# Splitting the first batch of a fused attention and MoE kernel by tokens instead of by head pairs

## The chip, the cores and the metric

The kernel runs on one core of one Trainium2 chip. The metric is the device time of one execution in microseconds (us). A profiled run also gives its span, from the first to the last instruction, which is a little shorter than the time (333.3 us of span for a run of 335.13 us). On one core a run counts as slow when it is over 1.5% above the fastest run of the same kernel in the same series; slow runs enter no ratio here, but the medians quoted are over all runs.

The engines are written as in the profile: PE is the matmul engine (TensorE), PEld its weight loads, DVE is VectorE, ACT is ScalarE, POOL is GpSimd, SP is SyncE, which here only issues transfers.

## The reference, cut to what matters

Eight batches of eight heads attend over 576 tokens with a head size of 64. Half of the heads use a local mask (the last 32 positions), half a strided one (every 32nd position). The result, 4608 tokens of 512 columns, goes through two dense layers with a squared relu between them.

```python
scores = scale * np.matmul(q, k.transpose(0, 1, 3, 2))
mask_local   = (rel >= 0) & (rel < stride)                      # heads 0..3
mask_strided = (rel >= 0) & (pos[None] % stride == pos[:, None] % stride)   # heads 4..7
attn = softmax(where(mask, scores, -1e9))
x = np.matmul(attn, v).transpose(0, 2, 1, 3).reshape(4608, 512)
h = x @ w_in                 # 512 -> 2048
g = relu(h) ** 2
y = g @ w_out                # 2048 -> 512
```

## The kernel before

A *unit* is one batch and one pair of heads: units 0 and 1 of each batch are local, 2 and 3 strided. The dense layers take chunks of 512 tokens. One *group* of the first layer is four matmuls of 128 by 128 by 512 into one PSUM bank, a relu on ACT, and a square on DVE:

```python
def mm1(c, ff, kks=range(4), order=range(4), pool=None):
    ...
    for kk in kks:
        nc.tensor.matmul(ph, w_in_b[:, kk, 128 * ff:128 * (ff + 1)],
                         xt[kk][:, 512 * c:512 * (c + 1)],
                         start=(kk == order[0]), stop=(kk == order[-1]))
    if kks[-1] != order[-1]:
        return
    r = r_pool.tile([128, 512], BF16, name="r")
    nc.scalar.activation(r, ph, AF.Relu)
    later(1, lambda: nc.vector.tensor_tensor(g[:, ff, :], r, r, op=ALU.mult))
```

The first batch is special, because nothing else can run beside its attention. Its four units are computed for all 576 tokens, and the matmuls of three groups are slipped into the end of that attention, unit by unit (`NP = 3`):

```python
first_order = (0, 2, 3, 1)
...
order = [(t(a, "q"), 0), (t(a, "k"), 2), (S_(a), 4), (t(b, "q"), 1), ...
         (n(c), 0), (o(c), 0), (lambda: part((a, b), (0,)), 0), (n(d), 0), (o(d), 0),
         (lambda: part((a, b), (1, 2)), 0), (lambda: part((c,)), 0), (lambda: part((d,)), 0)]
```

(`t` transposes q or k, `S_` makes scores, `n` sums of exponentials, `o` the products with V; the numbers are idle matmuls meant to keep PE's clock up.)

All loads that convert from fp32 to bf16 on the way are issued by POOL in its program order, between its other work. Here all four quarters of w_in are issued in one go, after two casts:

```python
load_v_first()                # V of batch 0, converted by the DMA
cast_qk_local(1, pool2)       # two casts on POOL
for i in range(4):
    load_w_in(i)
...
loads(1)
```

`loads(1)` starts with a one-element copy that reads the third quarter of w_in, the *gate*. It holds batch 1's loads back until that quarter has landed. Behind the gate, in POOL's order, come two casts before the second quarter of w_out and two more before the third:

```python
w_out(0); load_qk_str(u + 2); cast_qk_local(u, pool2)
w_out(1); cast_qk_local(u + 1, pool2); load_qk_str(u + 3)
w_out(2); ...
```

The softmax here doesn't subtract the row's maximum and nothing guards it: scores larger than these inputs give would overflow.

## Time and profile before

| | before |
|---|---|
| time, three runs | 323.25 us median (322.17 to 323.48) |
| span of the profiled run, granted clock | 319.6 us, 0.984 |
| PE busy | 300.0 us (94%) |
| DVE, ACT, POOL busy | 170.7, 163.7, 87.8 us |
| gate opens (third quarter of w_in has landed) | 23.31 us |
| first-layer groups run without other work between them from | 25.55 us |
| second layer starts | 37.29 us |
| third quarter of w_out first used | 48.26 us |

PE is the bound over most of the span, so what can change the time is what lets PE start: the first 50 us. From the start of the second layer to the end the kernel before takes 319.6 - 37.29 = 282.3 us.

One line of the timeline (start, duration, engine, line, operation, tile and source, count) will matter: when POOL issues the four quarters of w_in.

```profile
11.36 3.01 POOL L202 DMA_DIRECT2D w_in_b<-in_moe_w_in_dram  x4
```

POOL is done with all of w_in at 14.4 us, and the software queue (the DMA queue of the loads that POOL issues; SP's is the hardware queue) has work without a break up to the gate.

### The profile page before, as it was taken

To read this page: it belongs to the slowest core of one execution; us is meant where nothing else is said; L and a number is where in the kernel's file an instruction comes from. 1 tells how busy PE (TensorE), PEld (TensorE's weight loads), DVE (VectorE), ACT (ScalarE), POOL (GpSimd) and SP (SyncE) were. 2 spreads that over 40 slices of the span, in tenths; PEclk is the share of its full clock that TensorE was granted. 3 is DMA by queue.
4 is the path that set the end of the run, shared out by engine and by line. 5 is a ranking of instruction groups with operands and counts; after the bars stand their busy time and mean duration, and the time that the engine had idled before them with its cause. 6 is when DMAs were issued, how large, how long until landed. Compare 5 with 4: busy or idle time off the path is not lost.

```text
span 319.6 us, 6138 instructions
## 1 busy us (share of the span) xinstructions
PE 300.0 (94%) x2322; PEld 149.5 (47%) x2364; DVE 170.7 (53%) x414; ACT 163.7 (51%) x337; POOL 87.8 (27%) x114
## 2 busy tenths in 40 slices
PE   7789978898999989999999999999999999999995
PEld 3454545444555444444444444444444444444442
DVE  6476463677956975676585557555555222222200
ACT  4576644477655755554554455545543443434311
POOL 8605472473930713271182015000000000000000
PEclk9859999999999999999999999999999999999999
DMA  7999999999999999999797677000411110000021
GB/s 182 172 205 227 221 155 251 186 328 208 198 162 210 197 212 182 212 242 188 183 211 167 145 159 133 35 33 33 53 51 36 55 42 36 33 33 35 35 96 66
DMA packets 87220, 44.79 MB, mean 140 GB/s; under 512 B 71768, under 2 KB 80376, under 8 KB 87000
## 3 DMA queue, kind: packets, MB, share of 16 engines
q1 hardware_dynamic: 77448, 34.81, 53.3%
q0 software_dynamic: 9744, 9.60, 18.9%
q8 instruction: 18, 0.29, 0.4%
q14 instruction: 10, 0.08, 0.1%
HBM read 36.89 MB, written 12.98 MB: 156 GB/s over the span
## 4 chain that ended last, share of the span: by engine, by line
PE 78%; DMA 9%; DVE 6%; ACT 3%; issue 2%; POOL 1%; SPq 0%; ACTq 0%; POOLq 0%
PE ph L412 33%; PE py L430 26%; PE ph L430 10%; PE pt L359 3%; PE pt L277 3%; DMA w_out_b<-in_moe_w_out_dram 3%; DMA q_st<-in_q_dram 3%; DMA kT_s<-in_k_dram 3%; DVE xt L396 1%; PE pt L388 1%; DVE e L288 1%; PE pt L233 1%; DVE g_sb L419 1%; ACT r L418 1%; ACT e L282 1%
## 5 line engine op out<-in xcount | busy, mean ns | idle before, releaser
L412 PE MATMUL ph<-xt,w_in_b 128*128 128x512 bf16 x557 | 143.3, 380 | 3.3 <-DVE xt L396 1.9
L418 ACT ACTIVATE r<-ph 128x512 bf16<-128x512 f32 x143 | 85.3, 597 | 99.5 <-PE ph L412 96.2
L419 DVE TENSOR_TENSOR g_sb<-r 128x512 bf16<-128x512 bf16 x144 | 71.2, 496 | 102.4 <-ACT r L418 101.9
L430 PE MATMUL py<-w_out_b,g_sb 128*128 128x512 bf16 x383 | 100.2, 379 | 1.3 <-issue 0.5
L430 PEld LDWEIGHTS <-g_sb 128*128 128x128 bf16 x576 | 52.9, 98 | 60.8 <-issue 4.3
L412 PEld LDWEIGHTS <-w_in_b 128*128 128x128 bf16 x576 | 51.7, 98 | 54.5 <-issue 1.3
L282 ACT ACTIVATE e<-pt 128x288 bf16<-128x288 f32 (+1 forms) x128 | 48.8, 406 | 17.0 <-PE pt L277 16.9
L430 PE MATMUL ph<-w_out_b,g_sb 128*128 128x512 bf16 x166 | 40.7, 379 | 1.9 <-DMA w_out_b<-in_moe_w_out_dram 1.2
L181 POOL CAST vl<-vl_st 128x768 bf16<-128x768 f32 x14 | 12.4, 886 | 60.2 <-DMA vl_st<-in_v_dram 58.1
L359 PEld LDWEIGHTS <-e 128*128 128x128 bf16 (+1 forms) x392 | 21.0, 97 | 15.6 <-DVE e L288 0.5
L371 DVE TENSOR_TENSOR x_s<-pt,rinv 72x384 bf16<-72x384 f32 (+1 forms) x42 | 21.4, 509 | 1.4
L288 DVE TENSOR_TENSOR e<-e,mask_str 72x576 bf16<-72x576 bf16 x32 | 18.0, 563 | 5.9 <-ACT e L282 5.6
L122 POOL CAST q_l<-q_st 96x768 bf16<-96x768 f32 x15 | 13.0, 865 | 21.9 <-DMA q_st<-in_q_dram 19.4
L288 DVE TENSOR_TENSOR e<-e,mask_loc 128x576 bf16<-128x576 bf16 x32 | 16.7, 523 | 1.7 <-ACT e L282 1.7
L122 POOL CAST k_l<-k_st 96x768 bf16<-96x768 f32 x15 | 13.3, 885 | 13.9 <-DMA k_st<-in_k_dram 13.8
L370 DVE RECIPROCAL rinv<-pt 96x6 f32<-96x6 f32 (+2 forms) x70 | 12.9, 184 | 7.8 <-PE pt L359 7.8
L434 ACT COPY y<-py 128x512 f32<-128x512 f32 x25 | 14.7, 587 | 4.0 <-PE py L430 4.0
L371 DVE TENSOR_TENSOR x_l<-pt,rinv 96x384 bf16<-96x384 f32 x28 | 15.5, 553 | 1.8 <-DMA xt<-x_l 0.9
L434 ACT COPY y<-ph 128x512 f32<-128x512 f32 x11 | 6.4, 586 | 19.4 <-PE ph L430 19.4
L197 POOL CAST vs<-v_st 72x1024 bf16<-72x1024 f32 x14 | 15.4, 1126 | 1.6 <-DMA v_st<-in_v_dram 1.3
L359 PE MATMUL pt<-vs,e 72*128 72x65 bf16 x224 | 13.7, 193 | 0.1
L182 POOL CAST vl<-vl_st 32x640 bf16<-32x640 f32 x14 | 11.9, 850 | 0.9
(77 smaller groups left out, 154.2 us busy)
## 6 DMA issues: line engine op xcount, KB each, us to landing
out_dram<-y SPq DMA_DIRECT2D x36, 256.0 KB, 2.0
vl_st<-in_v_dram SPq DMA_DIRECT2D x28, 144.0 KB, 4.0
v_st<-in_v_dram SPq DMA_DIRECT2D x14, 288.0 KB
q_st<-in_q_dram SPq DMA_DIRECT2D x8, 288.0 KB, 7.1
k_st<-in_k_dram SPq DMA_DIRECT2D x8, 288.0 KB, 7.9
q_st<-in_q_dram SPq DMA_DIRECT2D x16, 144.0 KB, 3.8
k_st<-in_k_dram SPq DMA_DIRECT2D x16, 144.0 KB, 5.9
w_in_b<-in_moe_w_in_dram POOLq DMA_DIRECT2D x4, 512.0 KB, 9.4
```

Of the source, the lines that this page charges most:

```text
L122: copy(t.rearrange("p j h d -> p h j d"), s[name + "f"].rearrange("p h (j d) -> p h j d", j=6))
L197: (copy or nc.gpsimd.tensor_copy)(t[:, :, 0:D], s["vf"].rearrange("p h (j d) -> p (h j) d", d=D))
L282: nc.scalar.activation(e[0:kn, lo:lo + S // 2], banks[row][half][0:kn, 0:S // 2], AF.Exp, scale=scale)
L288: nc.vector.tensor_tensor(x, x, m.to_broadcast([kn, n, w]), op=ALU.mult)
L359: nc.tensor.matmul(po[:, n - n0, :], e[0:kn, pos(n):pos(n) + 128], rhs[0:kn, src(n), 0:D + 1], start=True, stop=True)
L370: nc.vector.reciprocal(rinv[0:w, 0:m], po[0:w, 0:m, D:D + 1])
L371: nc.vector.tensor_tensor(x, po[0:w, 0:m, 0:D], rinv[0:w, 0:m].to_broadcast([w, m, D]), op=ALU.mult)
L412: nc.tensor.matmul(ph, w_in_b[:, kk, 128 * ff:128 * (ff + 1)], xt[kk][:, 512 * c:512 * (c + 1)], start=(kk == order[0]), stop=(kk == order ...
L418: nc.scalar.activation(r, ph, AF.Relu)
L419: later(1, lambda: nc.vector.tensor_tensor(g[:, ff, :], r, r, op=ALU.mult))
L430: nc.tensor.matmul(py, g[:, ff, 128 * j:128 * (j + 1)], w_out_b[:, ff, :], start=(ff == 0), stop=(ff == 15))
L434: nc.scalar.copy(y, py)
```

## The change

The intent is to get dense work to PE earlier. Batch 0 is cut into two halves of 288 tokens. The first half's attention is done for all heads; then each of the first layer's 16 groups is computed for tokens 0 to 255 only, with the attention of the second half placed between these half groups. A second sweep of 16 half groups does tokens 256 to 511. Local V of batch 0 is no longer converted by the DMA: it is loaded as it is (fp32, packets of 256 B) on SP's hardware queue and cast on POOL. The diff, cut to its core:

```diff
-    def mm1(c, ff, kks=range(4), order=range(4), pool=None):
+    def mm1(c, ff, kks=range(4), pool=None, lo=0, hi=512):
...
+        ph = phs[ff][:, lo:hi]
...
-        nc.scalar.activation(r, ph, AF.Relu)
+        nc.scalar.activation(r[:, lo:hi], ph, AF.Relu)
...
     def first_steps():
-        (all four pairs, 576 tokens each, three groups slipped in)
+        (first half's attention, local and strided heads)
+        m = lambda ff, kks=range(4), pool=None: mm1(0, ff, kks, pool, 0, CH)   # CH = 256
+        ... m(3); tick(); half_T("l", 1, "q", V); m(4); tick(); half_T("l", 1, "k", V); m(5) ...
+        ... m(14); tick(); half_O("s", 1); m(15); tick()
...
-    load_v_first()
-    cast_qk_local(1, pool2)
-    for i in range(4):
-        load_w_in(i)
+    load_local_half(0)
+    load_v_local_half(0)             # plain, on SP
+    load_local_half(1)
+    load_v_local_half(1)             # plain, on SP
...
+    load_v_str_a()
+    load_w_in(0)
+    cast_v_local_half(0, nc.gpsimd.tensor_copy)
+    load_str_half(1, "q")
+    load_str_half(1, "k")
+    load_w_in(1)
+    for name in "qk":
+        cast_half(1, name, nc.gpsimd.tensor_copy)
+    load_v_str_all()
+    cast_v_local_half(1, nc.gpsimd.tensor_copy)
+    load_w_in(2)
+    load_w_in(3)
+    first_steps()
     for t in vl_sts:
         nc.vector.memset(t[0:32], 0.0)      # one-time memsets, formerly ahead of the attention
...
     for ff in range(16):
-        add(0, 1, ff) if ff >= NP else add(0, 0, ff)
+        add(0, 0, ff)                       # kind 0 is now: mm1(0, ff, lo=CH)
```

## The prediction

> **What bounds the kernel now.** I began with the page of the profile.
>
> ```profile
> span 319.6 us, 6138 instructions
> ...
> PEclk9859999999999999999999999999999999999999
> DMA  7999999999999999999797677000411110000021
> ```
>
> A slice is 8 us. After the first three slices PE runs at full clock; the DMA engines are at 90% or more from slice 2 to slice 19, 150 us. The table of windows has PE busy 4.95 of 5 us from 30 to 35 and 78.6 of 80 from 120 to 200, so once work flows there is nothing to win; what the change can shorten are the first 50 us.
>
> ```profile
> 10.00:15.00 5.00, 3.61 (x65) 2.30 (x65) 3.07 (x10) 2.59 (x7) 3.77 (x5) 0.79 1.67 164
> 15.00:20.00 5.00, 4.24 (x63) 2.90 (x61) 3.59 (x9) 4.11 (x13) 0.00 (x0) 0.50 1.24 205
> 20.00:25.00 5.00, 4.67 (x45) 2.52 (x44) 3.48 (x8) 2.71 (x7) 1.42 (x3) 0.69 1.14 193
> 25.00:30.00 5.00, 4.75 (x23) 2.07 (x22) 3.54 (x7) 3.87 (x7) 3.06 (x5) 1.00 1.09 226
> ```
>
> (Stretch, length, busy of PE, PEld, DVE, ACT, POOL, granted clock, DMA share, GB/s.) From 13 to 24 us PE looks busy but has half its clock; dense first-layer work begins near 24. That invites the change: less attention before the first dense matmul.
>
> Next the timeline and the chain of waits, to see what happens to work that comes earlier.
>
> ```profile
> 10.90 0.31 PEld L233 LDWEIGHTS <-kT_s 72*128 72x128 bf16 x8 [1.36 <-DMA kT_s<-in_k_dram]
> ...
> 23.31 0.18 POOL L111 CAST q_st<-w_in_b 1x1 f32<-1x1 bf16 x1 [8.94 <-DMA w_in_b<-in_moe_w_in_dram]
> ```
> ```profile
> 48.26 1.02 PE L430 MATMUL ph<-w_out_b,g_sb 128*128 128x512 bf16 x4 [1.23 <-DMA w_out_b<-in_moe_w_out_dram]
> ```
> ```profile
> 24.43 9.16 DMA q_st<-in_q_dram
> ...
> 37.43 10.79 DMA w_out_b<-in_moe_w_out_dram
> ```
>
> This is a second chain beside PE: the third quarter of w_in lands at 23.3 and opens the gate for batch 1's loads; q_st takes 9.16 us; GpSimd casts and only then, at 37.43, issues the third quarter of w_out, which lands at 48.22. PE has by then run out of work and waits 1.23 us. **A gain on PE before 48 us beyond 1.2 us is lost in this wait, unless w_out lands earlier too.** From gate to landing are 24.9 us, in none of which the change takes out a transfer.
>
> **What the Trainium skill says.** "TensorE: Matmul & The Clock Gate", section "What's actually happening": the clock is halved after an idle window of about 3.4 us and returned after a busy one. The trace agrees: PE waits from 8.6 to 10.9 but for one short burst, and has 0.50 from 13 to 23. "DMA: Bandwidth & Descriptors", section "Issuing engines are not separate DMA queues": DMAs of all issuers share the same 16 engines. The trace agrees: 205 GB/s with the software queue alone (15 to 20), 226 with both (25 to 30), so moving a load to the other queue does not add its bandwidth. Same page, "Why small descriptors are slow": small packets carry a fixed cost; measured below. "VectorE: DVE Perf Modes", in the section on the TRN2 errata, gives ScalarE from PSUM 172 cycles plus one per column at 1.2 GHz: 570 ns for 512 columns, 383 for 288. The trace has 597 and 406-413, so I take about 380 ns for 256.
>
> **The change part by part: DMA.** Four windows of the DMA view give the price of a packet (packets, MB, share): 3 to 4 us, 10 to 12, 16 to 24, 57 to 58.
>
> ```profile
> q1 hardware_dynamic: 202, 0.29, 107.0%
> ```
> ```profile
> q0 software_dynamic: 2221, 0.32, 230.4%
> ```
> ```profile
> q0 software_dynamic: 1637, 1.62, 122.5%
> ```
> ```profile
> q1 hardware_dynamic: 761, 0.19, 137.3%
> ```
>
> Dividing 16 engines times the window by the packets: 79 ns of one engine for a 1.5 KB hardware packet, 14 for a 128 B software packet, 78 for a 1 KB software packet, 21 for a 256 B hardware packet alone. Beside software traffic (33 to 34 us: 450 hardware and 125 software packets) the last comes to (16000 - 125*78)/450 = 14 ns.
>
> Before, up to the gate: local q, k 768 packets * 79 = 61 us; strided q, k 576, strided v 288, three quarters of w_in 1536, together 2400 * 78 = 187 us; local v 96*24 + 32*23 = 3040 * 14 = 43 us. Sum 291/16 = 18.2 us; from 2 us, plus some 2.5 us from a packet's start to its landing, 22.7 against 23.3 measured. After: q, k the same 61; local v plain, 2944 packets of 256 B * 14 to 21 = 41 to 62; software 2400 plus 144 for the second copy of the first half's strided v (2 * 36 rows * 2 heads) = 2544 * 78 = 198. Sum 300 to 321, or 18.8 to 20.1 us. **The gate opens 0.5 to 1.9 us later; I take 1.3**, and w_out follows: 49.5.
>
> **PE, ACT and DVE before the first dense matmul.** The first strided transposes still wait for k near 11: it sits behind as many hardware bytes. From there, with rows of before: transposes and copy 0.4 + 0.5, scores 0.6, two exp 0.8, mask 0.45, sums 0.7, two Ln 0.7, Exp 0.7, product and two multiplies 1.2 + 0.8, in all 6.9 us, so xt of the first tokens is whole near 18, against 24.1 before (13.2 us after k). That is 6 us sooner. But half of the attention is still to do. In this phase ACT has 16 relu * 0.38 = 6.1, eight exp * 0.41 = 3.3, four Ln * 0.355 and two Exp * 0.68 = 2.8, sum 12.2 us. PE has 64 matmuls of 256 columns at half of 216 ns = 6.9 and about 5 of attention, at half clock for the first few. DVE has about 10. And w_in comes in quarters 2.6 us apart (512*78/16 = 2.5): the second near 21, the third 24.6, the fourth 27.2. Group 12 needs the fourth; behind it four groups and the last sums and products, 4 to 5 us: the phase ends near 32.
>
> Then 16 half groups of 0.43 us. With two PSUM buffers, matmul 0.43 + relu 0.38 + two handovers of about 0.07 gives 0.475 a group, so PE no longer hides relu as it did with 0.86 against 0.60. Also the one-time memsets (1.5 + 0.28 + 0.28 + 0.24 + 0.59 = 2.9 us of DVE, formerly at 1.5 to 4.7 us) now come after the first phase in DVE's order, which four r buffers hide mostly. Twelve groups take 5.7: batch 1's first transposes at 32 + 5.7 + about 0.3 = 38.0, against 34.83. Of the first layer 4*0.43 = 1.7 us is then left, against 4*0.865 = 3.46: PE is 3.2 - 1.7 = 1.5 us behind. It reaches the w_out wait at 47.03 + 1.5 = 48.5 and w_out is there at 49.5. The end moves by the later of them: 49.5 - 48.26 = +1.3 us. Extra weight loads of the split (64) run beside matmuls: nothing.
>
> **Rivals.** (1) *The intended gain*: dense work starts 6 us sooner and all of it stays, 317 us. For it: 11 us at half clock and PE gaps before 24. Against: half the attention is only moved behind, and the 1.23 us wait at 48.26 catches what is won. I give this a small chance. (2) *w_out earlier*: if both queues together move more than I price, the gate may open 1 to 2 us sooner, PE's gain then shows up to that amount: 321. (3) *First phase paced worse*: GpSimd issues the last quarters of w_in only after two casts that wait for the second half's q, k and v; were the software queue to run dry, every later landing moves by it. I estimate the issue near 17 us and the queue full until 20, so 3 us of margin. With PE in order behind late w_in, and half clock for longer, 328 to 330. (4) *Nothing*: the gate unchanged, 323.
>
> **Range and chances.** The base is 323.25 + 1.3 = 324.5. The gate's price is known to about 1 us, the phase's end to 2-3 us, and PE may be late but not usefully early, so the range leans up: 320.5 to 329.5. Faster by 2% needs 6.5 us, more than the chain leaves: 0.08. Slower by 2% needs over 329.7: 0.11. Within: 0.81.
>
> **What will show it.** Right: first 256-column matmuls at 16 to 19 us; gate at 24 to 25.5; w_out's third quarter at 49 to 51 with a PE wait on it or PE just arriving; the rest of the span, from there to the end, within 0.5 us of 271.4 (319.6 - 48.2). ACT as what PE waits for in the second half's groups. Wrong: a gate before 23 us, which would mean that transfers of the two queues overlap better; a w_out wait gone with an earlier end, which would mean that the chain through q_st and the casts got shorter; or a gap of PE over 2 us before the fourth quarter of w_in, or a tail longer than before because kTl is now one tile and its users wait for one another.

## The result, and the profile after

The changed kernel is slower: **334.51 us median (330.75 to 335.13, four runs)** beside 322.71 us for the kernel before in the same series (321.65 to 323.48, four runs). The ratio is 1.036, with a 95% interval of 1.029 to 1.043. Here and below a ratio compares fast runs alone, so it is not quite the ratio of the medians quoted. The predicted range ended at 329.5.

The page of the profile after: its first line and the two rows of 40 slices for the granted clock and the DMA engines.

```profile
span 333.3 us, 6576 instructions
...
PEclk9975999999999999999999999999999999999999
DMA  8979999998999999998699888300130001000021
```

A slice is now 8.3 us. The third slice of DMA has dropped below 80% (7), and the low clock has moved to the third and fourth slices. Both rows point at 17 to 33 us. The milestones say how much was lost and by when:

| | before | after |
|---|---|---|
| gate opens | 23.31 | 29.52 |
| second layer starts | 37.29 | 51.13 (+13.8) |
| third quarter of w_out first used | 48.26 | 60.81 |
| from the second layer's start to the end | 282.3 | 282.2 |

All of the 13.7 us between the two spans are lost before the second layer starts. What follows costs the same in both.

The chain of waits (start, duration, what) goes back to one transfer:

```profile
2.20 6.81 DMA vl_st<-in_v_dram
9.03 13.93 DMA vl_st<-in_v_dram
23.10 0.77 POOL g_sb L333
23.87 5.53 DMA w_in_b<-in_moe_w_in_dram
29.45 1.03 PE ph L566 x4
```

It reads as a sentence. SP issues the last 128 KB of the second half of local V only at 9.03 us, because that load shares its semaphore (a counter on which engines wait) with a load of the first half that landed at 9.01. They need 13.93 us; POOL casts them; only then does POOL issue the third quarter of w_in; 5.5 us later PE can use it. The timeline after, with the idle time before each piece and its releaser in brackets, shows who stood still for this:

```profile
22.28 0.61 PE L566 MATMUL ph<-xt,w_in_b 128*128 128x256 bf16 x4 [2.12 <-DMA w_in_b<-in_moe_w_in_dram]
23.10 0.83 POOL L333 CAST g_sb<-vl_st 128x768 bf16<-128x768 f32 x1 [7.37 <-DMA vl_st<-in_v_dram]
23.87 1.54 POOL L210 DMA_DIRECT2D w_in_b<-in_moe_w_in_dram  x2
29.45 1.03 PE L566 MATMUL ph<-xt,w_in_b 128*128 128x256 bf16 x4 [1.46 <-DMA w_in_b<-in_moe_w_in_dram]
29.52 0.18 POOL L119 CAST q_st<-w_in_b 1x1 f32<-1x1 bf16 x1 [3.45 <-DMA w_in_b<-in_moe_w_in_dram]
42.01 1.51 DVE L803 MEMSET vl_st<- 32x768 f32 x2
45.30 0.66 ACT L572 ACTIVATE r<-ph 128x256 bf16<-128x256 f32 x2 [1.91 <-DVE g_sb L573]
45.73 4.87 PE L566 MATMUL ph<-xt,w_in_b 128*128 128x256 bf16 x36 [1.69 <-ACT r L572]
51.13 1.03 PE L584 MATMUL ph<-w_out_b,g_sb 128*128 128x512 bf16 x4
55.24 0.18 POOL L119 CAST q_st<-w_out_b 1x1 f32<-1x1 bf16 x1
60.81 1.03 PE L584 MATMUL ph<-w_out_b,g_sb 128*128 128x512 bf16 x4
```

There are three things to see. POOL stood for 7.37 us, and the last two quarters of w_in were issued at 23.87, where the kernel before had issued all four by 14.4 us. PE waited twice for w_in, 2.12 us for the second quarter and 1.46 us for the third; before, nobody but the gate waited for it. The second quarter had been issued at 12.50 us, before POOL stood, so only the second of these waits belongs to POOL. Later PE stood 1.69 us behind ACT, which stood behind DVE, which at 42 us was busy with the memsets that the change had moved there. And the last two lines reverse the prediction's end: the third quarter of w_out had landed by 55.24 and PE came to it only at 60.81, without a wait. PE itself was last.

The windows (stretch, length, busy of PE, PEld, DVE, ACT, POOL, granted clock, DMA share, GB/s) show the hole in the transfers and the clock:

```profile
15.00:20.00 5.00, 3.76 (x31) 2.70 (x25) 2.28 (x6) 1.90 (x5) 0.73 (x2) 0.66 1.23 203
20.00:25.00 5.00, 2.59 (x40) 1.80 (x39) 2.62 (x6) 1.09 (x3) 1.90 (x3) 0.81 0.50 80
25.00:30.00 5.00, 3.54 (x39) 2.10 (x35) 1.62 (x5) 1.78 (x5) 1.26 (x3) 0.50 1.06 161
```

From 20 to 25 us the DMA engines moved 80 GB/s, where before they moved 193: the software queue ran dry from about 22 us. In steps of 1 us from 20 us the rate was 207, 122, 55, 14, 0 and 18 GB/s, and back at 165 from 26 to 27. In the same 5 us PE was busy for 2.59 us, and after it the clock was halved.

Why did 128 KB take 13.93 us? The DMA view after, for 14 to 15 us and then for 19 to 20 us (packets, MB, share of 16 engines):

```profile
q0 software_dynamic: 154, 0.16, 92.4%
q1 hardware_dynamic: 156, 0.04, 30.2%
...
q0 software_dynamic: 193, 0.19, 113.5%
q1 hardware_dynamic: 58, 0.01, 10.8%
```

From 14 to 15 us V's packets (q1, 256 B) and the converting loads' packets (q0, mostly 1 KB) were taken one for one, so V got a fifth of the bytes. It was so from 13 to 15 and from 16 to 17 us; from 12 to 13 and from 15 to 16 V got more (305 packets beside 121, 329 beside 169), and from 17 us ever fewer. The Trainium skill, "DMA: Bandwidth & Descriptors", section "Queues, rings and completion order", says that each DMA engine goes round the queues it has work for packet by packet; its packet is a bunch of descriptors, so it is not quite the profile's packet. The count at 14 us agrees with turns by packet and not by byte. The later count does not: at 19 us V got 58 of 251, from 20 to 22 us 10 or 11 a microsecond. The packed trace shows where the last ones were. Each load counts up its semaphore in sixteen steps, and of the last V load fifteen steps had come by 20.41 us, the sixteenth at 22.95. I read a step as one share of the load: then one share of sixteen was late, and 2.5 of POOL's 7.37 us went to it; V's packets of that time ran some 0.1 us apart, each for 31 ns. The two loads ahead show the same (fifteen steps by 14.95 and 17.08, the last at 16.54 and 19.65). In other runs this share was less late: in e6 below the steps ended at 20.41 and 20.46, in e8 at 20.62 and 21.30. Why it was late is open; the trace does not name the engine of a packet.

### The profile page after: what moved, and what is told of

Same layout as the page of the kernel before. It is cut to its first block, busy times and chain, and to the rows that moved or that the text cites. A ratio compares the mean times of both kernels' runs of the same rounds, so it can differ in the third digit from the quotient of the medians.

```text
span 333.3 us, 6576 instructions
## 1 busy us (share of the span) xinstructions
PE 309.1 (93%) x2532; PEld 157.3 (47%) x2532; DVE 170.1 (51%) x426; ACT 165.2 (50%) x351; POOL 90.7 (27%) x119
## 4 chain that ended last, share of the span: by engine, by line
PE 79%; DMA 8%; DVE 7%; ACT 2%; issue 1%; SPq 0%; POOL 0%; ACTq 0%; DVEq 0%; POOLq 0%
PE ph L566 34%; PE py L584 26%; PE ph L584 10%; DMA vl_st<-in_v_dram 6%; PE pt L513 3%; PE pt L285 3%; DMA w_in_b<-in_moe_w_in_dram 2%; DVE g_sb L573 2%; PE pt L542 1%; PE pt L241 1%; DVE xt L550 1%; DVE e L296 1%; ACT r L572 1%; DVE x_s L525 1%; DVE xt L494 0%
## 5 line engine op out<-in xcount | busy, mean ns | idle before, releaser
L566 PE MATMUL ph<-xt,w_in_b 128*128 128x512 bf16 (+1 forms) x636 | 152.1, 366 | 9.5 <-DMA w_in_b<-in_moe_w_in_dram 3.6
L572 ACT ACTIVATE r<-ph 128x512 bf16<-128x512 f32 (+1 forms) x159 | 88.2, 555 | 111.3 <-PE ph L566 107.3
L573 DVE TENSOR_TENSOR g_sb<-r 128x512 bf16<-128x512 bf16 (+1 forms) x160 | 73.2, 461 | 116.3 <-ACT r L572 115.0
L584 PE MATMUL py<-w_out_b,g_sb 128*128 128x512 bf16 x400 | 102.7, 379 | 0.0
L566 PEld LDWEIGHTS <-w_in_b 128*128 128x128 bf16 x640 | 58.6, 100 | 60.3 <-DMA w_in_b<-in_moe_w_in_dram 5.5
L290 ACT ACTIVATE e<-pt 128x288 bf16<-128x288 f32 (+1 forms) x112 | 43.2, 406 | 11.8 <-PE pt L285 11.7
L584 PE MATMUL ph<-w_out_b,g_sb 128*128 128x512 bf16 x176 | 42.5, 379 | 0.0
L296 DVE TENSOR_TENSOR e<-e,mask_str 72x576 bf16<-72x576 bf16 x28 | 15.7, 561 | 2.4 <-ACT e L290 2.4
L205 POOL CAST vs<-v_st 72x1024 bf16<-72x1024 f32 x14 | 16.5, 1199 | 0.5
L296 DVE TENSOR_TENSOR e<-e,mask_loc 128x576 bf16<-128x576 bf16 x28 | 12.5, 448 | 1.5 <-ACT e L290 1.5
```

Source lines behind the costliest of these rows:

```text
L205: (copy or nc.gpsimd.tensor_copy)(t[:, :, 0:D], s["vf"].rearrange("p h (j d) -> p (h j) d", d=D))
L290: nc.scalar.activation(e[0:kn, lo:lo + S // 2], banks[row][half][0:kn, 0:S // 2], AF.Exp, scale=scale)
L296: nc.vector.tensor_tensor(x, x, m.to_broadcast([kn, n, w]), op=ALU.mult)
L572: nc.scalar.activation(r[:, lo:hi], ph, AF.Relu)
L573: later(1, lambda: nc.vector.tensor_tensor(g[:, ff, lo:hi], r[:, lo:hi], r[:, lo:hi], op=ALU.mult))
L584: nc.tensor.matmul(py, g[:, ff, 128 * j:128 * (j + 1)], w_out_b[:, ff, :], start=(ff == 0), stop=(ff == 15))
```

## The experiments

The theory after reading the trace, called the **queue theory**: the plain loads of V and their cast's place in POOL's order hold back w_in, and everything follows from it. Its rivals: the **half groups** (PE passes through all of w_in some 8 us sooner than before, so it meets the landings, and a half group is less efficient); the **memsets**; the **half clock**; and the **split itself** (the second half's attention comes too late, whatever the queue does). Fifteen kernels were run, each with runs of the kernel before. Between calls only the ratios compare; the spread of the ratios is 0.5 to 1.0% either way, and several of the differences below are no larger. All kernels gave correct results. "Second layer" below is the start of the second layer in that kernel's profile.

| kernel | median us | beside before | ratio (95%) | gate | second layer |
|---|---|---|---|---|---|
| after | 334.51 | 322.71 | 1.036 (1.029 to 1.043) | 29.5 | 51.1 |
| e1 cast last | 331.75 | 321.28 | 1.022 (1.014 to 1.029) | 26.8, slow run | 48.0, slow run |
| e2 memsets early | 330.96 | 321.28 | 1.029 (1.024 to 1.035) | 29.9 | 50.1 |
| e4 V by converting DMA | 330.01 | 321.28 | 1.027 (1.021 to 1.033) | 25.7 | 46.1 |
| e5 = e4 and e2 | 329.63 | 324.00 | 1.019 (1.013 to 1.025) | 25.9 | 45.3 |
| e6 pairs | 331.43 | 324.00 | 1.022 (1.013 to 1.032) | 26.9 | 44.7 |
| e7 = e5 and pairs | 329.03 | 324.00 | 1.019 (1.011 to 1.026) | 27.1 | 45.8 |
| e8 warm | 332.82 | 324.00 | 1.029 (1.024 to 1.035) | 28.8 | 48.6 |
| e9 = e5 without half groups | 326.84 | 321.00 | 1.020 (1.015 to 1.024) | 25.9 | 42.2 |
| e11 = e7 and w_in first | 326.31 | 321.00 | 1.019 (1.011 to 1.026) | 22.4 | 44.4 |
| e12 after without half groups | 329.88 | 321.00 | 1.028 (1.023 to 1.034) | 28.1 | 46.5 |
| e13 = e9 and w_in first | 326.64 | 321.52 | 1.013 (1.007 to 1.020) | 22.6 | 43.5 |
| e3 before, w_in late | 327.55 | 321.28 | 1.016 (1.009 to 1.023) | 29.8, slow run | 38.8, slow run |
| e10 before, w_out earlier | 325.01 | 321.00 | 1.016 (1.009 to 1.022) | 23.8 | 36.9 |
| e14 before, plain V | 326.35 | 321.52 | 1.012 (1.002 to 1.023) | 27.7 | 39.4 |
| e15 before, plain V cast last | 322.51 | 321.52 | 1.002 (0.994 to 1.010) | 24.0 | 39.0 |

### e1: the cast of V after the last quarters of w_in

```diff
-    cast_v_local_half(1, nc.gpsimd.tensor_copy)
     load_w_in(2)
     load_w_in(3)
+    cast_v_local_half(1, nc.gpsimd.tensor_copy)
```

> Changed kernel, but GpSimd's cast of the second half of local V comes after the issue of the third and fourth quarters of w_in. Queue theory (GpSimd stood from 15.73 to 23.10 for that V and could not issue w_in, so the gate opened at 29.5): quarters three and four are issued near 16.5, the gate opens at 24.5 to 26, PE's waits on w_in (12.6 us of PEld and PE together) shrink to under 4, and the time falls by 5 to 8 us, to 327 to 330. Phase theory (the first phase is slow by itself: PE in order behind ACT and DVE, half clock): gate just as early, time down by 2 us at most.

Measured: fast runs 327.79 and 329.48, ratio 1.022. Two of its four runs were slow (334.02 and 341.87), the profiled one among them, so its milestones count only as an order of events: w_in was issued at 16.35, 7.5 us sooner than after, and the gate opened at 26.8. One line moved in POOL's order takes some 1.5 of the 3.6 points away; the two intervals just touch, at 1.029. The rest stays.

### e2: the memsets before the attention

```diff
     nc.vector.memset(mask_la[0:32, 0], 0.0)
+    (memsets of vls, vss and es, here on DVE)
     load_w_in(0)
...
-    first_steps()
     for t in vl_sts:
-        nc.vector.memset(t[0:32], 0.0)
-    (memsets of vls, vss and es)
+        nc.gpsimd.memset(t[0:32], 0.0)
+    first_steps()
```

> Changed kernel, but the one-time memsets stand before the first phase (those of the V staging on GpSimd). Tail theory: PE's gap at 44.0 to 45.7, when DVE did nothing but memsets, goes, time down by 1.5 to 2 us, as PE and not w_out is what comes last there (w_out's third quarter lands at 55.2, PE uses it at 60.8). Queue theory alone, with the loads as what comes last: no change (under 0.5 us).

Measured: the second layer starts at 50.05, 1.1 us sooner than after, with the gate as late as there (29.9). The ratio, 1.029, fits, but its interval overlaps that of after. So the memsets cost about 1 us by the traces, less than the gap of 1.69 us that they showed and the 1.5 to 2 us that I had expected.

### e3: the kernel before with w_in held back

```diff
-    for i in range(4):
-        load_w_in(i)
+    load_w_in(0)
+    load_w_in(1)
+    busy = singles.tile([128, 768], FP32, name="busy")
+    nc.gpsimd.memset(busy, 0.0)
+    for _ in range(12):
+        nc.gpsimd.tensor_copy(busy, busy)
+    load_w_in(2)
+    load_w_in(3)
```

> The kernel before, but GpSimd does about 8 to 10 us of idle copies between the issue of the second and third quarters of w_in. Nothing of the token split is in it. Queue theory: the gate moves from 23.3 to about 28 to 30, w_out's third quarter from 48.2 to 53 to 55, PE's wait on w_out grows by the same, time up by 4 to 6 us over before. If the loads have slack that PE's order hides: up by under 2 us.

Measured: 1.016. The fast runs were some 5 us above those of before, as the queue theory had it (4 to 6). POOL issued the last quarters at 24.47, as late as after, and the gate opened as late. This is the queue's lateness without any of the rest of the change, and it makes under half of the loss. The profiled run was the slow one (331.92; the others 325.69 to 328.21); in it PE waited 2.06 us for the second quarter of w_out at 46.72, and the third landed at 53.1 instead of 48.2. This is the second chain of the prediction at work, in the kernel for which it was read.

### e4: the second half of V by converting DMA

```diff
-    load_v_local_half(1)
...
-    cast_v_local_half(1, nc.gpsimd.tensor_copy)
+    for i in range(NL // 2, NL):
+        k0 = QL * i - 32
+        nc.gpsimd.dma_start(out=vl0[:, i], in_=v[0, 0:4].rearrange("h s d -> s h d")[k0:k0 + 128])
     load_w_in(2)
```

> Changed kernel, but the second half of local V is loaded by casting software DMAs as before, straight into place, and GpSimd casts nothing. Queue theory: like e1_cast_last, gate at 24.5 to 26.5, time 327 to 330. Phase theory: 332 to 335.

From its timeline:

```profile
17.59 1.52 POOL L210 DMA_DIRECT2D w_in_b<-in_moe_w_in_dram  x2
```

The issue came 6.3 us sooner than after, the gate 3.8 us sooner (25.68), the second layer 5.1 us sooner (46.05). The ratio of 1.027 moved less than the milestones (its profiled span is 5.4 us under that of after), and its interval overlaps that of after. With the queue mended PE is still 8.8 us behind the kernel before, and the third quarter of w_out, landed at 50.5, stands ready 5 us before PE uses it. The queue theory is right about the gate and does not suffice for the time.

### e5: e4 and e2 together

> e4_v_cast_dma and e2_memsets_early together. If the late w_in and the late memsets are separate costs on PE's path they add: gate near 25.7, third quarter of w_out used by PE at 54 to 54.5 (55.9 in e4_v_cast_dma), time 1.5 to 2 us below e4_v_cast_dma, 328 to 328.5. If w_out (50.5 in e4_v_cast_dma) is what PE waits for: no gain over e4_v_cast_dma.

The edit is that of e4 and that of e2. Measured: 1.019, 329.63 us where I had expected 328 to 328.5; second layer at 45.27. The phase from the first use of w_in's third quarter (25.81) to the end of the second half's attention (36.65) took 10.8 us, the second sweep 8.6 us (its first microseconds at a low clock, 0.72 from 35 to 40). Both are longer than the prediction had them (7.4 and 8.3), the first by much.

### e6 and e7: two half groups share a bank, a relu and a square

```diff
+    def mm1_pair(ff):
+        g, o = gs[0], 256 * (ff % 2)
+        if ff % 2 == 0:
+            phs["pair"] = ph_tile()
+        for kk in range(4):
+            nc.tensor.matmul(phs["pair"][:, o:o + 256], ... xt[kk][:, 256:512], ...)
+        if ff % 2 == 0:
+            return
+        (one relu and one square of 512 columns)
...
-            groups.append(lambda: mm1(0, i, lo=CH))
+            groups.append(lambda: mm1_pair(i))
```

> Changed kernel, but the second halves of two first-layer groups share one PSUM bank, one relu and one square of 512 columns. Tail theory (two 256-column groups take 1.07 us because relu 0.38, its wait and two PSUM buffers stand in a row, against 0.87 of PE work): two groups take 0.87 to 0.92, the sixteen groups end 1.5 to 2.5 us sooner and the time falls by as much, to 332 to 333. If they are bound by weight loads or PE itself: no change.

> All three repairs. If they add, PE comes to the third quarter of w_out near 52 and the time is 325.5 to 327, still above before, because the gate is still 2.4 us later than before (25.7 against 23.3) and the first phase still runs PE in order behind ACT and DVE. If the token split itself were sound, this version would reach before or beat it.

e6 changes the second sweep alone; e7 adds it to e5. The timeline of e6:

```profile
37.80 6.38 PE L580 MATMUL ph<-xt,w_in_b 128*128 128x256 bf16 x57 [0.27 <-DVE xt L494]
```

Fourteen half groups in 6.38 us are about 0.45 each, the rate of PE, where half groups with a relu each took 1.07 us for two (the chain of waits after has them at 46.80, 47.87 and 48.94). The gap behind the memsets was gone too. But V happened to land sooner in this run (its cast at 20.61 instead of 23.10, without the late share), so part of the 6.4 us by which the second layer came sooner is not the edit's. e7, for which I had expected 325.5 to 327 us, took 329.03, with the same ratio of 1.019 as e5. Its gate opened 1.2 us later than that of e5 and its second layer 0.6 us later. The pairs make the sweep as fast as expected; what they win in time is not resolved.

### e8: idle matmuls that hold the clock

```diff
         half_T("l", 1, "q", V)
+        warm(8)
         m(4)
...
         half_mask("l", 1, 0)
+        warm(8)
         m(8)
```

> Changed kernel with eight idle 512-column matmuls before group 4 and eight before group 8, where PE waits for w_in, so that the clock should not be halved after the waits (it was 0.50 from 25 to 30 us). Clock theory: granted clock 1.0 from 24 to 33 us, groups 8 to 15 done 2 to 3 us sooner, time 331.5 to 333. Queue theory: the loads decide, time within 1 us of the changed kernel's 334.5, or up by up to 1.

Measured: the clock was 1.00 from 25 to 35 us, where after has 0.50 and 0.67; V landed 1.7 us sooner. From the third quarter's first use (28.69) to the end of the phase (39.19) were 10.5 us, against 11.75 after. The half clock costs this phase about 1 us by these traces; the edit also puts 16 idle matmuls in PE's way. It is not what makes it long: PE stands behind masks on DVE, sums and products in program order, and the same waits appear at full clock.

### e9 and e12: no half groups

```diff
         half_O("s", 0)
-        m = lambda ff, kks=range(4), pool=None: mm1(0, ff, kks, pool, 0, CH)
-        (sixteen half groups between the steps of the second half)
+        (the steps of the second half, one after the other)
...
-        add(0, 0, ff)
+        add(0, 1, ff)
```

> e5_queue_memsets, but no half groups: the second half's attention follows the first half's at once, then sixteen first-layer groups of 512 columns. Sweep theory (the half groups make PE walk through all of w_in some 8 us earlier than full groups do, so that the landing of its third quarter stands in PE's path, and everything behind it - rest of the phase, the second sweep - follows): the second half's attention is done near 27, groups of 0.87 us run from there, the second layer starts at 40.5 to 42 (45.3 in e5_queue_memsets), PE comes to the third quarter of w_out at about 51, time 324 to 326. If the token split's small matmuls or its chain of copies are what costs: second layer at 44 or later, time 328 or more.

> The changed kernel with its late w_in (third and fourth quarter issued near 23) and late memsets, only without half groups: attention of the second half at once, then groups of 512 columns. Sweep theory: gate still at 27 to 30, but PE needs that quarter only after eight full groups, so it no longer waits there; second layer at 42 to 45 (51.1 in the changed kernel), w_out at 53 to 55 becomes what comes last, time 326 to 329 against 334.5. If the late w_in by itself costs PE everything: 332 to 335.

e12 makes this edit in the changed kernel, e9 in e5. e12, with V's cast still in the way, had its second layer at 46.47, 4.7 us sooner than after, and this although PE stood 4.67 us for one copy on POOL that V's cast held up. By the traces the half groups thus cost more than they gave; the ratios (1.028 against 1.036, with overlapping intervals) do not settle it, and e12 missed what I had expected (second layer at 42 to 45). e9 was the best of the token-split kernels so far at 42.23. By the traces that is 3.0 us less than e5; the ratios (1.019 and 1.020) do not show it, and I leave the size open. It just missed what I had expected (second layer by 42, 324 to 326 us). e9's timeline and windows say what remains:

```profile
17.12 0.60 PE L369 MATMUL pt<-ident,w_out_b 36*128 36x36 bf16 x14 [1.60 <-DMA w_out_b<-in_q_dram]
...
21.39 1.15 PE L416 MATMUL pt<-qT,kT_s 64*72 64x36 bf16 x32 [2.06 <-POOL kT_s L618]
...
25.78 14.37 PE L566 MATMUL ph<-xt,w_in_b 128*128 128x512 bf16 x56
...
42.23 1.03 PE L584 MATMUL ph<-w_out_b,g_sb 128*128 128x512 bf16 x4
```
```profile
20.00:25.00 5.00, 3.45 (x72) 2.97 (x73) 1.55 (x5) 2.81 (x8) 1.33 (x3) 0.50 1.46 195
25.00:30.00 5.00, 4.76 (x29) 1.85 (x26) 2.33 (x5) 1.98 (x5) 2.36 (x5) 0.53 0.90 189
```

The first two lines show why dense work starts no sooner: PE waits 1.60 us for the second half's strided q and 2.06 us for one small copy that stands in POOL's order behind casts and issues. Dense work starts at 25.78, the kernel before's at 25.55. But before had done three of the sixteen groups inside the attention. Twelve matmuls of 0.216 us are 2.6 us. And e9 runs at half clock until about 29.7 us (0.65 in the microsecond from 29 to 30), where before has 1.00: from 25.78 that costs 3.9 / 2 = 2.0 us. Together 0.2 + 2.6 + 2.0 = 4.8 us, and 42.23 - 37.29 is 4.94.

### e10: the kernel before with w_out's third quarter issued sooner

```diff
         w_out(1)
+        w_out(2)
         cast_qk_local(u + 1, pool2)
         if b < XB:
             load_qk_str(u + 3)
-        w_out(2)
```

> The kernel before, but the third quarter of w_out is issued before GpSimd waits for the second local pair of batch 1. If the wait at 48.26 alone holds PE there: the quarter lands 2 to 6 us sooner, PE's wait of 1.2 us goes, time down by 1 us. If batch 1's own loads are what follows next, they come later by the 2.6 us of that quarter and the time stays or rises by 1 to 2.

Measured: 1.016, slower by more than the 1 to 2 us that I had allowed for. This was the wait that the prediction put at the end of its sum. Issued sooner it only moved: the third quarter was used at 47.04 without it, then PE waited for the fourth:

```profile
52.53 1.02 PE L430 MATMUL ph<-w_out_b,g_sb 128*128 128x512 bf16 x4 [1.84 <-DMA w_out_b<-in_moe_w_out_dram]
```

and the next gate, that of batch 2's loads, opened at 50.02 instead of 48.27. A PE wait of 2.2 us on batch 2's attention came later.

### e11 and e13: the first three quarters of w_in ahead of the second half's V

```diff
     cast_v_local_half(0, nc.gpsimd.tensor_copy)
+    load_w_in(1)
     load_str_half(1, "q")
     load_str_half(1, "k")
-    load_w_in(1)
+    load_w_in(2)
     for name in "qk":
         cast_half(1, name, nc.gpsimd.tensor_copy)
-    load_v_str_all()
...
     load_w_in(3)
+    load_v_str_all()
```

> e7_queue_memsets_pairs, but the first three quarters of w_in go ahead of the second half's strided V and of its local V. Sweep theory: the third quarter lands near 23.5 to 25 (27.1 in e7_queue_memsets_pairs), group 8 and everything behind it on PE move by the same 2 to 3 us, time 326 to 327. If the rest of the phase is bound by ACT and DVE or by the later V: no change, 328 to 330.

> e9_tokens_only with the first three quarters of w_in ahead of the second half's V, and the copy of the first half's strided keys on DVE, not behind GpSimd's casts. Gate theory (what is left of the 6 us in e9_tokens_only is the gate, 25.9 against 23.3, and the loads that hang on it): gate at 22 to 23.5, third quarter of w_out at 47.5 to 49, PE there at 50 to 52, time 322 to 325 against 326.8. If the token split itself costs the rest: 326 or more in spite of the earlier gate.

e11 is e7 with this order. e13 is e9 with nearly this order (strided V stays ahead of the fourth quarter) and with the small copy that had blocked PE moved from POOL to DVE. The timelines of e11 and e13:

```profile
22.43 0.18 POOL L119 CAST q_st<-w_in_b 1x1 f32<-1x1 bf16 x1 [0.68 <-DMA w_in_b<-in_moe_w_in_dram]
...
44.37 1.03 PE L598 MATMUL ph<-w_out_b,g_sb 128*128 128x512 bf16 x4
```
```profile
19.34 0.60 PE L369 MATMUL pt<-ident,w_out_b 36*128 36x36 bf16 x14 [3.25 <-DMA w_out_b<-in_q_dram]
```

In both the gate opens *earlier* than in the kernel before (22.4 and 22.6 against 23.3), w_out is there at 48.5 and 48.9, and the second layer is still 7.1 and 6.2 us late. That settles that neither the gate nor w_out holds these versions: PE itself is late. In e13 the second half's strided q, which now comes behind the second quarter of w_in, makes PE wait 3.25 us, and V another 0.74. Its sum closes as e9's does: dense work from 27.33 is 1.8 us later than before, the twelve matmuls are 2.6, and half clock up to about 31 us (0.50 to 30, 0.90 from 30 to 35) is about 1.8; together 6.2 of 6.17. e13 has the lowest ratio of the token-split kernels, 1.013, and is still slower than the kernel before; at 326.64 us it missed the 322 to 325 that the gate theory gave. e11's earlier gate won nothing that the ratio shows (1.019, as e5 and e7).

### e14 and e15: the kernel before with plain loads of local V

```diff
     load_qk_local(1, nc.sync)
+    load_v_local(0, nc.sync)
+    load_v_local(1, nc.sync)
...
     cast_qk_local(1, pool2)
+    for i in range(2):                        # e14: here
+        (two casts of V on POOL)
     for i in range(4):
         load_w_in(i)
+    for i in range(2):                        # e15: here
+        (two casts of V on POOL)
```

> The kernel before, with nothing but batch 0's local V loaded plain on the hardware queue and cast on GpSimd ahead of the issue of w_in. Queue theory: the 256-byte packets share engines one to one with 1 KB packets and land at 13 to 17, GpSimd stands until then, w_in is issued at 15 to 20 and not at 11.4, the gate moves from 23.3 to 26.5 to 30, time up by 3 to 6 us. If plain loads are harmless without the token split: within 1 us of before.

> e14_before_plain_v, but the casts stand behind the issue of w_in. Queue theory: gate within 1.5 us of 23.3, time within 2 us of before; PE may wait a little for V at its first product (16.3 before). If it is the traffic of plain loads and not GpSimd's order: as slow as e14_before_plain_v.

This is one part of the change alone, in two orders. The timelines of e14 and of e15:

```profile
13.54 0.82 POOL L573 CAST g_sb<-vl_st 128x768 bf16<-128x768 f32 x1 [3.13 <-DMA vl_st<-in_v_dram]
...
17.14 3.02 POOL L202 DMA_DIRECT2D w_in_b<-in_moe_w_in_dram  x4
```
```profile
11.03 3.02 POOL L202 DMA_DIRECT2D w_in_b<-in_moe_w_in_dram  x4
```

With the casts ahead of w_in the loads are issued 6 us later, the gate opens at 27.66, and the time is 326.35 us beside 321.52 (fast runs 326.01 to 326.58), slower by 1.2%. With the same loads and the same casts, only behind w_in, it is 322.51 us, the same as before to within 1%. The plain loads themselves cost nothing that shows; the place of their casts in POOL's order does. (The intervals of the two ratios overlap; the fast runs do not, 326.01 to 326.58 against 321.38 to 325.68, and the gates, 27.66 and 24.00, are apart.) (e15's profiled run was its slowest of four, 325.68 us, so its second layer at 39.0 overstates it.)

## Why the prediction was wrong

What was right: PE's first matmuls of 256 columns came at 16.4 us (predicted 16 to 19); the second chain from the gate through POOL's casts to w_out exists and passes on a delay in the kernel before (e3); and what follows the second layer's start costs the same (282.2 against 282.3 us). Counted as the prediction counted, from the third quarter of w_out, the rest was 272.5 us and not within 0.5 of 271.4.

The direction of the prediction's end, a little slower, was right; the size was wrong by 10 us, and two steps failed.

**The step that failed first is the third rival's margin: "I estimate the issue near 17 us and the queue full until 20, so 3 us of margin."** The issue came at 23.87 us. I had named the right mechanism and given it the wrong size (the 328 to 330 us that the rival was given were short as well), because I priced V's 256 B packets by engine time alone (14 to 21 ns each) and let the second half of V land with the rest of its bytes. Next to the software queue they came in turns, in three of the microseconds from 12 to 17 one for one of four times its size, one share of the last load came 2.5 us behind the others, and POOL stood 7.37 us. The queue held a little longer than the 20 us of the prediction, to about 22, which was not enough. With that the gate, predicted at 24 to 25.5, opened at 29.5. The prediction listed "a gap of PE over 2 us before the fourth quarter of w_in" as a sign of this failure; the gap was 2.12 us, before the second quarter; as that one was issued before POOL stood, the sign came true for another reason (PE was there before the load), and the gap of 1.46 us before the third quarter is the one that belongs here. That this order of POOL is a cause is shown by e14 against e15 (1.2% against nothing, in the kernel before) and, less sharply, by e1 and e4 in the kernel after (1.036 down to 1.022 and 1.027).

**The second step is PE's account, "the phase ends near 32 ... It reaches the w_out wait at 47.03 + 1.5 = 48.5".** In the prediction's own terms the second layer would have started near 40.3: batch 1's first transposes at 38.0, then 1.7 us of first layer, a transpose and the next pieces. That is already 3 us behind the 37.29 of before, and not 1.5: the prediction took 3.46 us of first layer as left at 34.83 in the kernel before, and its timeline has two groups there (eight matmuls from 35.30), 1.73 us. With this put right PE would have come to w_out near 50, behind its 49.5, and the forecast would have been about half a microsecond higher. The second layer started at 51.13. The sum of what was mis-sized:

| term | predicted | measured | off by |
|---|---|---|---|
| third quarter of w_in usable by PE | 24.6 | 29.45 | +4.9 |
| from there to the end of the first phase | 7.4 | 11.75 | +4.4 |
| second sweep up to the second layer | 8.3 | 9.9 | +1.6 |
| second layer starts | 40.3 | 51.1 | +10.8 |

The first term is the queue again. The second is a different mistake: I added up what ACT, PE and DVE had to do (12.2, 12 and 10 us), but let the landing of the fourth quarter (27.2) and 4 to 5 us behind it set the phase's end. The fourth quarter held nothing up: group 12, which needs it, began at 34.95 without a wait. Groups 8 to 11 with the steps between them took 5.5 us from 29.45, where the prediction had 2.6, and from group 12 to the end it was 6.3. PE worked in program order (at 37.75 it had stood 1.04 us for a mask on DVE, with half groups behind it), and so, with half groups in between, every mask, sum and product of the second half became something for the next half group to stand behind. Even with the queue mended (e5) and at full clock (e8) this phase took 10.5 to 10.8 us. The third term holds the memsets, which the four r buffers were to "hide mostly" (about 1.1 us by e2), and the half groups, which took 0.535 us each and not 0.475; in pairs with one relu (e6) they took about 0.45.

**The claim that w_out sets the end fell with these.** "The end moves by the later of them" named w_out at 49.5 and PE at 48.5. w_out came at 55.2 and PE at 60.8. In all versions of the changed kernel that were profiled in the fast state the second layer's start plus 280.6 to 283.8 us is the span of the profiled run, whether the gate opened at 22.4 or at 29.9. The spread of 3.2 us is as large as some of the steps compared, but it does not follow the gate. So the path of PE itself was the bound in them.

**What the token split itself does.** With the queue, the memsets and the half groups all taken out (e9, e13) the kernel is still 1.3 to 2.0% slower, and the traces account for its second layer to within 0.2 us: the dense work starts no earlier than before (25.8 and 27.3 against 25.55), three groups that the kernel before had slipped into its attention now stand behind it (2.6 us), and the first 4 us of dense work are at half clock (about 2 us). For the first and the last I take PE's waits before 22 us to be the cause: strided q and the copy on POOL in e9 (1.60 and 2.06 us), strided q in e13 (3.25 us). The wait for the copy is POOL's order once more and not the token split, and no run has both the copy on DVE and strided q early; so how much of the 1.3 to 2.0% is the split itself is not shown. This is arithmetic on traces; nor did I run a version of e9 in which the clock alone was repaired, so the 2 us are argued, not shown. Also open: how the 8.9 us between after (51.1) and e9 (42.2) divide exactly between the queue, the memsets and the half groups. Repaired alone, the queue is worth 5.1 us (e4), the memsets 1.1 (e2) and the half groups 4.7 (e12). The sum, 10.9, is more than 8.9: they overlap, since half groups are what makes PE meet w_in while it lands.

One of the prediction's readings of the Trainium skill was also looser than it said: PE's stretch of waiting before the half clock, 8.6 to 10.9 us, is 2.3 us long with a burst in it, so the trace of before does not show an idle window of 3.4 us.

No version beat the kernel before.

## What to carry to other kernels

Before a load is moved to another queue, look at what stands behind its consumer in program order: a cast that waits for a slow load also delays every transfer that the same engine issues after it, and in e14 it was this order, not the load, that cost the time. When two queues share the DMA engines, do not price a load by its bytes alone: ask how many packets wait beside it, and that its last share may come later than the rest (2.5 us here). And work that is cut finer to start sooner also reaches its next operand sooner; ask where that operand's landing is before counting the head start as a gain.

## What the Trainium skill lacked or had wrong

- "DMA: Bandwidth & Descriptors", section "Queues, rings and completion order", gives turns by packet, with packets of many descriptors. It does not say what that does to a queue of small packets beside one of large packets. Here 156 packets of 256 B went beside 154 of mostly 1 KB in one microsecond (0.04 against 0.16 MB), then 58 beside 193, and at the end some 10 a microsecond, so that a load of 128 KB took 13.93 us to land, its sixteenth share 2.5 us behind the fifteenth. This section does not explain the falling share.
- I found on no page a measured cost of converting loads that stand in program order behind a cast which waits for data. Here POOL waited 7.37 us for a load before a cast, and the DMA engines fell to 80 GB/s from 20 to 25 us: the software queue ran dry from about 22 us, while the next converting loads stood behind that cast.
- "TensorE: Matmul & The Clock Gate", section "What's actually happening": nothing wrong was found. It says that the number of matmuls at half clock differs from run to run and puts the penalty of the ramp at under 1% of a typical span; the estimate from e9, for a half clock in mid-kernel (2.0 us of 325), is of that size. The changed kernel's four fast runs had mean granted clocks of 0.98, 0.974, 0.974 and 0.995 at 335.13, 334.24, 334.79 and 330.75 us, 1.2% between the last and the mean of the others; one run at 0.995 does not show that the clock is the reason.
